# Wider exps, and a kernel's side work placed by a built-in time model: attention beside a state-space layer on one core

## The chip, the cores and the metric

One core of one Trainium2 chip. The metric is the device time of one launch in microseconds (us), median of several runs. The engines are TensorE (PE in the profile; PEld its weight loads), VectorE (DVE), ScalarE (ACT), GpSimd (POOL) and SyncE (SP), which in this kernel issues nearly all DMAs. SPq, PEq and so on are the engines' instruction queues.

Kernel before: 1026.12 us.

## The reference

```python
x = A_x                                              # 1 x 2048 x 512, bf16
g = sigmoid((x * gate_w).sum(-1, keepdims=True))
a = attention(x, wqkv, wo)                           # 32 heads of 16, softmax over 2048 keys, then @ wo
b = s4_conv(x, A, B, C, log_dt, Dskip)               # 512 channels x 128 complex states, length 2048
return g * a + (1 - g) * b
```

Attention is dominated by the exps: 32 x 2048 x 2048 of them, on 128 partitions 1,048,576 columns. ScalarE does them all. The convolution (called the SSM below) is done in blocks of 64 steps: tables of powers (VectorE), block states ("S stage", TensorE), a scan over 32 blocks (VectorE), outputs ("y stage", TensorE). Its operands travel through HBM between the stages.

## The kernel before

The kernel is built in Python: a recorder (`Prog`) takes instructions in the order given to each engine and works out the semaphores. Engines run their own list strictly in that order. Attention is the frame; the SSM, the projections and the output product are generators whose pieces are put between its steps.

```python
def qk(q):                       # scores: 4 matmuls of 32 rows, into two 2-bank PSUM buffers of three
    slots = [(SC[((4 * q + j) // 2) % 3], (4 * q + j) % 2) for j in range(4)]
    ...
def ex(h):                       # one exp over two banks, 1024 columns
    op("ACT", lambda a: a.activation(ET(1024 * e, [[1, 1024]]), sc(0, [[1, 1024]]), AF.Exp, scale=DH ** -0.5), ...)
...
def sload(blk):                  # a DMA, and the flags that later work waits for while the program is built
    yield ("AFTER", f"S{blk}", 2)
    ...
    sch.mark(f"sg{blk}")
...
    yield ("AFTER", f"sg{4 * qr + bl}", 12)      # scan: 12 steps (22 us) after its load was issued
    yield ("AFTER", f"qt{blk}", 3)               # S stage: 3 steps more after its Qt load
    yield ("AFTER", f"yl{u}", 5)                 # y stage: 5 steps after its loads
...
for q in range(NQ):              # the frame: 512 steps of two exps
    ex(2 * q); qk(q + 1); ex(2 * q + 1)
    rate = dict(PE=.62 if q > 50 else 1.0, DVE=1.65, POOL=1.8)     # budget of side work in this step, us
    pv(...)                      # products of exps with V
    sch.step(rate)
```

The softmax here doesn't subtract the row's maximum and nothing guards it: scores larger than these inputs give would overflow.

## Time and profile before

| part of the 1027.0 us span | us | read from |
|---|---|---|
| until the first exp | 20.0 | timeline of ScalarE |
| 1024 exps x 0.917 | 939.0 | length of an unbroken run of exps |
| gaps between exps (waits for scores) | 43.7 | waits of ScalarE |
| two square roots with four table loads | 6.4 | timeline |
| slower first exps after gaps, rest | 6.8 | what is left |
| after the last exp | 11.2 | timeline |

The page of the kernel before: busy time and share of the span, and the 40-slice rows of ScalarE's share and TensorE's granted clock in tenths.

```profile
span 1027.0 us, 16317 instructions
...
PE 740.6 (72%) x6617; PEld 195.9 (19%) x6617; DVE 626.7 (61%) x1356; ACT 959.0 (93%) x1041; POOL 3.6 (0%) x11
...
ACT  4899999999999998999997987999999999999995
...
PEclk7998998555556555657555665555555555557856
...
L550 ACT ACTIVATE ET<-SC 128x1024 bf16<-128x1024 f32 x1024 | 944.8, 1097 | 44.7 <-PE SC L433 43.7
```

ScalarE is the limit: 93% busy, and the exps are nearly all of it. The last line reads: 1024 exps, 944.8 us busy in total, 1097 ns from start to end of one (they overlap, so an unbroken run costs 0.917 us each), 44.7 us of idle time before them, 43.7 of it waiting for score matmuls (`SC`). The clock is half for most of the span.

The next views of the kernel before are waits (engine, what it waited for, us in total, times, longest): ScalarE's first line.

```profile
ACT ET L550 <- PE SC L433: 43.7, 37, 3.4
```

### The profile page before, as it was taken

The numbers are of one execution on the slowest core, as the hardware profiler recorded it, in microseconds if no ns is written. First come the engines' busy times: TensorE is split into PE (matmuls) and PEld (weight loads), VectorE is DVE, ScalarE is ACT, GpSimd is POOL, SyncE is SP. The second block draws the span as 40 slices with busy tenths as digits, with TensorE's granted clock in tenths as the row PEclk, the third lists the DMA queues.
The fourth block names the chain that finished last, engine by engine and source line by source line (L and its number), as shares of the span: only waits on it lengthen the run. The fifth ranks groups of instructions, "written<-read, shape, count | busy, mean of one in ns | idle before, by whom it ended". The sixth has DMA issues, their size and how long they took to land.

```text
span 1027.0 us, 16317 instructions
## 1 busy us (share of the span) xinstructions
PE 740.6 (72%) x6617; PEld 195.9 (19%) x6617; DVE 626.7 (61%) x1356; ACT 959.0 (93%) x1041; POOL 3.6 (0%) x11
## 2 busy tenths in 40 slices
PE   5876766766776666676665667888878888877665
PEld 1211111211111111111111112232322222311111
DVE  6737889997567897766897632112999971122111
ACT  4899999999999998999997987999999999999995
POOL 0000000000000000000000000000000000000000
PEclk7998998555556555657555665555555555557856
DMA  8610000006667205459104475458454444200000
GB/s 179 138 28 1 1 1 1 1 1 176 191 192 169 88 1 113 152 146 211 41 1 136 137 193 128 107 106 170 118 127 88 97 96 110 53 14 26 21 11 21
DMA packets 227403, 92.17 MB, mean 90 GB/s; under 512 B 191872, under 2 KB 215040, under 8 KB 225280
## 3 DMA queue, kind: packets, MB, share of 16 engines
q1 hardware_dynamic: 225600, 90.21, 35.5%
q10 hardware_dynamic: 1728, 0.92, 0.5%
q8 instruction: 52, 0.85, 0.4%
q14 instruction: 23, 0.19, 0.1%
HBM read 27.92 MB, written 35.65 MB: 62 GB/s over the span
## 4 chain that ended last, share of the span: by engine, by line
ACT 61%; DVE 21%; PE 12%; SPq 3%; issue 2%; DMA 1%; DVEq 0%; POOL 0%; POOLq 0%
ACT ET L550 60%; PE MB L433 6%; PE SC L433 4%; DVE G L887 3%; PE OA L433 2%; DVE s L885 2%; DVE s L882 2%; DVE s L880 2%; DVE SG L889 2%; DMA gm_sd<-Sst 1%; SPq L787 1%; DVE VE L516 1%; DVE OT L565 1%; DVE VE L481 1%; SPq L911 1%
## 5 line engine op out<-in xcount | busy, mean ns | idle before, releaser
L550 ACT ACTIVATE ET<-SC 128x1024 bf16<-128x1024 f32 x1024 | 944.8, 1097 | 44.7 <-PE SC L433 43.7
L433 PE MATMUL SC<-Qm,KT 32*128 32x512 bf16 x2048 | 289.2, 555 | 210.8 <-ACT ET L550 206.6
L433 PE MATMUL OA<-ET,VE 128*32 128x512 bf16 x2048 | 286.2, 563 | 0.1
L433 PEld LDWEIGHTS SC<-Qm,KT 32*128 32x128 bf16 x2048 | 54.5, 97 | 411.4 <-ACT ET L550 394.2
L433 PEld LDWEIGHTS OA<-ET,VE 128*32 128x32 bf16 x2048 | 53.8, 101 | 188.4 <-issue 183.8
L947 DVE CAST Yst<-MB 128x256 bf16<-128x256 f32 x32 | 13.5, 421 | 116.1 <-PE MB L433 116.1
L834 DVE CAST Sst<-MB 128x256 bf16<-128x256 f32 x64 | 27.0, 422 | 61.9 <-PE MB L433 51.6
L575 DVE TENSOR_TENSOR tt<-B,D 128x1024 bf16<-128x1024 bf16 x96 | 62.0, 687 | 1.2
L433 PE MATMUL MB<-Qt,X 64*32 64x256 bf16 x512 | 39.1, 397 | 31.5 <-DVE Sst L836 26.7
L565 DVE STREAM_TRANSPOSE OT<-OA 128x512 f32<-128x512 f32 x32 | 22.9, 714 | 62.4 <-PE OA L433 62.2
L887 DVE TENSOR_TENSOR G<-s,s 128x256 f32<-128x256 f32 x120 | 51.0, 425 | 4.1
L880 DVE TENSOR_TENSOR s<-G,MU 128x256 f32<-128x256 f32 x120 | 50.1, 417 | 0.1
L882 DVE TENSOR_TENSOR s<-G,MU 128x256 f32<-128x256 f32 x120 | 50.1, 418 | 0.0
L885 DVE TENSOR_TENSOR s<-s,SG 128x256 f32<-128x256 f32 x120 | 50.1, 418 | 0.0
L433 PE MATMUL MB<-Py,SG 128*32 128x64 bf16 x1024 | 44.3, 260 | 1.4 <-issue 1.4
L1036 DVE SCALAR_TENSOR_TENSOR fo<-MB,g,Yl 128x512 bf16<-128x512 f32 x13 | 9.7, 748 | 51.8 <-PE MB L433 51.8
L433 PE MATMUL MB<-Tt,X 64*32 64x64 bf16 x512 | 35.7, 269 | 3.3 <-DVE Yst L947 3.3
L889 DVE CAST SG<-G 128x256 bf16<-128x256 f32 x120 | 35.2, 294 | 4.1
L575 DVE TENSOR_TENSOR PT<-tt,tt 128x1024 bf16<-128x1024 bf16 x48 | 33.2, 692 | 1.6
L575 DVE TENSOR_TENSOR ft<-FP,L 128x1024 f32<-128x1024 f32 (+1 forms) x32 | 33.7, 1085 | 0.4
L810 DVE CAST Kst<-MB 128x512 bf16<-128x512 f32 x16 | 11.0, 689 | 36.9 <-PE MB L433 36.9
L433 PE MATMUL MB<-xT,Wk 128*128 128x512 bf16 x64 | 22.5, 440 | 15.2 <-DVE xT L1078 8.0
(115 smaller groups left out, 430.5 us busy)
## 6 DMA issues: line engine op xcount, KB each, us to landing
gm_ptd<-PT SPq DMA_DIRECT2D x16, 1024.0 KB, 5.0
Py<-gm_ptd SPq DMA_DIRECT2D x32, 512.0 KB, 4.6
gm_sd<-Sst SPq DMA_DIRECT2D x64, 128.0 KB, 2.4
gm_kpd<-Kst SPq DMA_DIRECT2D x16, 256.0 KB, 2.6
Tt<-gm_kpd SPq DMA_DIRECT2D x128, 32.0 KB, 3.7
gm_xrd<-in_A_x_dram SPq DMA_DIRECT2D x1, 2048.0 KB, 12.3
X<-gm_xrd SPq DMA_DIRECT2D x8, 256.0 KB, 4.8
gm_ytd<-Yst SPq DMA_DIRECT2D x32, 64.0 KB, 1.8
```

The lines of the kernel that those rows point to most:

```text
L433: op("PE", lambda t: t.matmul(out(), lhsT(), rhs(), start=start, stop=stop, skip_group_check=True, **kw), R, W)
L550: op("ACT", lambda a: a.activation(ET(1024 * e, [[1, 1024]]), sc(0, [[1, 1024]]), AF.Exp, scale=DH ** -0.5), [(sc, 0, h // 2), (sc, 1, h / ...
L565: op("DVE", lambda v: v.transpose(OT(o, [[1, 512]]), OA(0, [[1, 512]])), [(OA, 0, b)], [(OT, 0, b)])
L575: op(eng, lambda v: v.tensor_tensor(o(), a(), b_(), f), R, W)
L810: op("DVE", lambda v: v.tensor_copy(Kst(1024 * (blk % 2) + 63, [[P, 8], [1, T]]), MB(0, [[T, 8], [1, T]])), [(MB, 0, ('K', blk)), (Kst, "z ...
L834: op("DVE", lambda v, bank=bank: v.tensor_copy(Sst(512 * bank, [[256, 2], [1, 128]]), MB(0, [[256, 2], [1, 128]])), [(MB, 0, ('S', blk, ba ...
L880: op(e, lambda v: v.tensor_tensor(s2(0, [[128, 2], [1, 128]]), G(0, [[128, 2], [1, 128]]), MU(d0, [[0, 2], [1, 128]]), ALU.mult), key("G", ...
L882: op(e, lambda v: v.tensor_tensor(s3(0, [[128, 2], [1, 128]]), G(128, [[-128, 2], [1, 128]]), MU(D + d0, [[D, 2], [1, 128]]), ALU.mult), k ...
L885: op(e, lambda v, so=so: v.tensor_tensor(s2(0, [[128, 2], [1, 128]]), s2(0, [[128, 2], [1, 128]]), sg(so, [[RS, 2], [1, 128]]), ALU.add), ...
L887: op(e, lambda v: v.tensor_tensor(G(0, [[1, 256]]), s2(0, [[1, 256]]), s3(0, [[1, 256]]), ALU.add), [(s2, 0), (s3, 0)], [(G, 0)])
L889: op(e, lambda v, so=so: v.tensor_copy(sg(so, [[RS, 2], [1, 128]]), G(0, [[128, 2], [1, 128]])), key("G"), ks)
L947: op("DVE", lambda v: v.tensor_copy(Yst(r2 * 256, [[1, 256]]), MB(0, [[1, 256]])), ky, [(Yst, r2, u)])
```

## The change

Its intent: fewer, wider exps (three banks at a time, two buffers of three banks in place of three of two); side work placed by a time model in the builder that asks what is ready and fits before the next scores; dummy matmuls that keep TensorE's clock up; the first 24 tiles of exps kept in a spare buffer, so that scores need not wait for V; V's ones written by GpSimd; square roots by Newton steps on VectorE, so that ScalarE loads no other table. The diff is 1,656 lines; its core:

```diff
-    sb("ET", 7 * 1024)
+    sb("ET", NE * 1536)                 # NE = 6
+    sb("EX", NX * 1536)                 # NX = 18
...
-    for i in range(3):
-        B[f"SC{i}"] = Buf(f"SC{i}", "ps", 1024, FP32)
+    for i in range(2):
+        B[f"SC{i}"] = Buf(f"SC{i}", "ps", 1536, FP32)
...
+    def put(self, o):                   # the time model: when does o run on its engine?
...
+        t = self.free[eng]
+        for d, j in deps.items():
+            t = max(t, self.te[(d, j)] + (.03 if d == eng else LAT))
+        if o.dma:
+            self.free[eng] = t + .12    # time that issuing a DMA takes
+            e = t + o.c                 # time at which it has landed
...
+    def run(self, now, pe_end, dve_end, margin=.02):     # place ready work until the next scores are due
...
+    def keep(b):                        # a dummy: adds zeros to the open product
+        return mm(lambda: OA(0, [[1, 512]]), lambda: wm(0, [[1, P]]), lambda: wm(0, [[1, 512]]), [(wm, 0)], [(OA, 0, b)],
+                  False, False, c=.24)
...
-        yield ("AFTER", f"qt{blk}", 3)
...
-                yield ("AFTER", f"sg{4 * qr + bl}", 12)
+                yield ("AFTER", f"sg{4 * qr + bl}")
...
-            yield ("AFTER", f"yl{u}", 5)
+            yield ("AFTER", f"yl{u}")
...
+        while opened and sch.units < 3.2 and p.free["PE"] + .3 < lim:
+            put(keep((pvn - 1) // 16))
+            sch.units += 1
```

## The prediction

> **What bounds it now.** ScalarE. The page gives it 959.0 of 1027.0 us (93%), 944.8 of that in 1024 exps of 128x1024; the chain that ended last is 60% exps. In the timeline 52 exps in a row take 47.84 us: 0.917 us each. At 1.2 columns per ns (853 ns), about 64 ns of it are fixed (estimate). The rest of the span: the first exp starts at 19.98 us; the last ends near 1015.8 (tail 11 us); 44.7 us are idle before exps in 37 gaps, nearly all put down to the score matmuls (waits view); two square roots with four table loads of 1.28 us take 6.4 us.
>
> **What the change does.**
> 1. Exps of 1536 columns: 682, and one of 1024. At 1280 + 64 = 1.344 us each: 917 us, against 1024 x 0.917 = 939. Saves 22 us, all on the critical path. An exp after a gap costs up to 0.18 us more, so fewer gaps save 4 to 6.
> 2. Square roots on VectorE: ScalarE saves 6.4 us. VectorE gains some 22 operations of about 0.65 us (14 us), but loses the 7.53 us fill of V's buffer and a second pass over each S bank (64 x 0.41 us). It is 61% busy: off the path.
> 3. Head: the V fill holds VectorE from 3.2 to 10.7 us, so the copies of x and the decay inputs start late (ScalarE idles 7.15 us before the `ea` exp). With ones from GpSimd I expect the first exp at 14.5 to 15.5 us: saves about 5.
> 4. Gaps. The early ones (20 to 60 us, about 5 us) come from V projections ahead of scores; with 24 score tiles buffered, most go. Later ones (2.4 to 3.5 us before S-stage matmuls whose inputs or eviction are late; 1.1 to 1.7 us at state, output and projection work) come from in-order TensorE work that delays the next scores. A period becomes 1.344 us with 3 score matmuls, and only ready work is placed in it. The order of instructions shows SSM and output work ending by score 1638 of 2048 (before: 1976), so it makes no tail.
> 5. 1006 dummy matmuls hold the TensorE clock up. At 500 to 550 us the granted clock is 0.50 and 4 score matmuls take 0.61 us; at 50 to 150 us it is 0.9 and they take 0.39. The Trainium skill, "TensorE: Matmul & The Clock Gate", Part 1, says activity in 3.4 us windows lifts the clock from half to full; this trace agrees (stretch means 0.50 to 0.94). At half clock, scores, products and two dummies would need about 4 x 0.43 = 1.7 us per 1.344 us tile, dense enough to lift it. I expect a mean clock above 0.85 and TensorE no bottleneck.
>
> **Sum.** First exp 15 + exps 917 + gaps 13 (4 to 40) + gate and restarts 1 + tail 11 = 957 us. Range 944 to 985. Chances: faster by over 2% 0.96, within 2% 0.03, slower 0.01.
>
> **What would show each step.** Exps: 683, busy 917 to 922 us, spacing 1.344; no square-root tables on ScalarE; first exp near 15 us; idle before exps under 20 us; clock over 0.85 in the middle; no SSM work in the last 200 us.
>
> **What would make it wrong.** The clock falling although dummies run (1.7 us tiles); an optimistic time model whose late DMAs or evictions block TensorE in order, so gaps stay at 40 us; GpSimd fills slowing VectorE in the head.

## More of the kernel before

```profile
PE SC L433 <- ACT ET L550: 206.6, 387, 3.5
PE MB L433 <- DVE Sst L836: 26.7, 19, 3.8
...
PE MB L433 <- DMA Qt<-gm_ptd: 2.1, 1, 2.1
```

TensorE waits mostly for ScalarE to free score buffers, which costs nothing. It waited for a DMA of the SSM once, for 2.1 us.

The view of one line, the `Tt` loads of the y stage in the kernel before: duration of an issue on SyncE (minimum/median/maximum, ns), who waited, and the time to landing.

```profile
L911 SPq DMA_DIRECT2D Tt<-gm_kpd x128: 583/617/1778, 603.9 to 881.5; - x128
...
who waited for it (us, times):
...
DMA to landing us min/median/max: 2.4/3.7/5.5
```

Each of these loads holds SyncE for 0.617 us. Nobody waited for one.

## The result

The changed kernel takes 1020.06 us (1019.48 to 1022.12, 4 runs) against 1024.96 us for the kernel before in the same job. The ratio is 0.9956 (95% interval 0.9933 to 0.9979). Ratios here and below are those on record, taken from the fast runs of one job, so not quite the ratio of the medians quoted. That is 0.4% faster, and 63 us above the prediction.

The page of the changed kernel, lines as before.

```profile
span 1017.4 us, 17925 instructions
...
PE 890.5 (88%) x7623; PEld 261.4 (26%) x7623; DVE 605.8 (60%) x1315; ACT 934.6 (92%) x694; POOL 8.4 (1%) x17
...
ACT  6999999999799999699999964899897999999996
...
PEclk9999989989799999889788965699795999999999
...
L681 ACT ACTIVATE ET<-SC 128x1536 bf16<-128x1536 f32 x665 | 902.8, 1598 | 68.1 <-PE SC L547 67.4
```

The exps are wider and fewer, the clock is high, the head is full. But idle time before exps grew from 44.7 to 68.1 us, and the holes in ScalarE's row lie in the middle, while the SSM runs.

The waits of the changed kernel, ScalarE's first line and TensorE's first four:

```profile
ACT ET L681 <- PE SC L547: 67.4, 74, 9.9
```

```profile
PE SC L547 <- ACT ET L681: 49.6, 120, 1.3
PE MB L547 <- DMA Tt<-gm_kpd: 24.5, 20, 9.4
PE MB L547 <- DVE Sst L937: 13.8, 12, 5.9
PE MB L547 <- DMA Qt<-gm_ptd: 5.9, 4, 2.3
```

TensorE now waits 30.4 us for DMAs of the SSM, where before it was 2.1. Its list is in order: while a y or S matmul waits for its load, the scores behind it wait too. The longest wait for `Tt`, 9.4 us, is the longest gap between exps, 9.9 us. Timeline of TensorE and ScalarE there (start, length, engine, line, what; in brackets the idle time before):

```profile
608.73 2.79 ACT L681 ACTIVATE ET<-SC 128x1536 bf16<-128x1536 f32 x2
...
619.39 0.26 PE L547 MATMUL MB<-Tt,X 64*32 64x64 bf16 x1 [9.42 <-DMA Tt<-gm_kpd]
...
620.78 0.61 PE L547 MATMUL SC<-Qm,KT 32*128 32x512 bf16 x3
...
621.44 1.45 ACT L681 ACTIVATE ET<-SC 128x1536 bf16<-128x1536 f32 x1 [9.92 <-PE SC L547]
```

And SyncE's own queue over the same stretch:

```profile
606.12 0.60 SPq L1050 DMA_DIRECT2D gm_ytd<-Yst  x1
606.77 7.34 SPq L960 DMA_TRANSPOSE SG<-gm_sd  x3
614.16 0.60 SPq L1004 DMA_DIRECT2D Py<-gm_ptd  x1
614.80 2.69 SPq L1009 DMA_DIRECT2D Tt<-gm_kpd  x4
```

SyncE was issuing three `SG` transposes for 7.34 us, then `Py`, then the four `Tt` loads for which TensorE stood still. Nothing is idle in this list: each issue follows the last within 0.1 us. The model had charged 0.12 us for each of them. The DMA engines were full too in these microseconds (a mean share of 1.02 from 600 to 621 us), but that is not what TensorE waited for: the four loads landed 3.5 to 4.6 us after their issues, as loads do elsewhere (below). TensorE had stood since 609.97 us, 4.8 us before the first of them was issued.

The second longest gap (6.3 us, ending at 433.5 us) comes from SyncE's list by way of another engine. Four `SG` transposes took SyncE 11.88 us; VectorE stood 7.92 us before a step of its scan that reads them, and the eviction (`Sst`) that an S matmul waited for stood behind that step in VectorE's list.

The view of the changed kernel's `Tt` line says who waited for those loads, and how fast they are:

```profile
L1009 SPq DMA_DIRECT2D Tt<-gm_kpd x128: 603/617/1674, 558.7 to 780.1; - x128
...
  PE MB L547: 24.5, 20
...
DMA to landing us min/median/max: 2.4/3.6/5.5
```

The loads are as quick as before, from issue to landing (3.6 against 3.7 us) and in the issue itself (617 ns in both). They were issued too late for the place that the program gives to the work on them.

| part of the span | before | predicted | after |
|---|---|---|---|
| until the first exp | 20.0 | 15 | 15.2 |
| exps | 939.0 | 917 | 917.5 |
| gaps between exps | 43.7 | 13 | 66.0 |
| square roots | 6.4 | 0 | 0 |
| first exps after gaps, gate, rest | 6.8 | 1 | 9.8 |
| after the last exp | 11.2 | 11 | 8.9 |
| sum | 1027.1 | 957 | 1017.4 |

The exps of the changed kernel are counted as 682 x 1.344 + 0.917 us; an exp after a gap shows 1.45 us, 0.106 more than 1.344, and 73 gaps of that are 7.7 of the 9.8. Of the 67.4 us in the view of waits, 1.4 lie before the first exp and are counted there. The gain on everything but the gaps and restarts, 35 us, is close to the predicted one. Of it, 25 us were given back as gaps and restarts in this profiled run.

I sorted the gaps by summing the timeline: 15 of 1 us or more sum to 40.1 us, 59 smaller ones to 27.3 (the one before the first exp included). (Before: 22 and 15, 37.0 and 6.8.) The small ones come mostly in trains behind a large one, as after the wait for `Qt` at 259 us:

```profile
259.64 0.65 PE L547 MATMUL MB<-Qt,X 64*32 64x256 bf16 x8 [2.31 <-DMA Qt<-gm_ptd]
...
264.59 1.03 PE L547 MATMUL OA<-wm 128*128 128x512 bf16 x2
265.56 0.61 PE L547 MATMUL SC<-Qm,KT 32*128 32x512 bf16 x3
266.10 0.62 PE L547 MATMUL OA<-ET,VE 128*32 128x512 bf16 x4
266.22 1.45 ACT L681 ACTIVATE ET<-SC 128x1536 bf16<-128x1536 f32 x1 [0.60 <-PE SC L547]
```

After the block the scores take 0.61 us (half clock) where they take 0.39 at full clock, and the two dummies `OA<-wm` in front of them take 1.03. A tile with scores, products and two dummies then needs about 2.05 us of TensorE from start to start (its matmuls overlap a little, so this is less than the sum of their lengths) against 1.45 us of ScalarE for an exp after a gap, so each such tile leaves a gap of 0.6 us until the clock is back.

### The profile page after: what moved, and what is told of

Read it like the earlier page. It is cut to its first block, busy times and chain, and to the rows that moved or that the text cites. A ratio compares the mean times of both kernels' runs of the same rounds, so it can differ in the third digit from the quotient of the medians.

```text
span 1017.4 us, 17925 instructions
## 1 busy us (share of the span) xinstructions
PE 890.5 (88%) x7623; PEld 261.4 (26%) x7623; DVE 605.8 (60%) x1315; ACT 934.6 (92%) x694; POOL 8.4 (1%) x17
## 4 chain that ended last, share of the span: by engine, by line
ACT 50%; PE 17%; DVE 15%; SPq 10%; DMA 5%; issue 1%; ACTq 0%; DVEq 0%
ACT ET L681 48%; PE OA L547 8%; PE SC L547 5%; PE MB L547 4%; SPq L1009 3%; DVE tt L712 3%; ACT EX L681 2%; DMA Qt<-gm_ptd 2%; SPq L960 2%; SPq L899 2%; DMA Tt<-gm_kpd 2%; DVE G L987 2%; DVE Sst L937 1%; DVE s L981 1%; DVE s L985 1%; DVE PT L712 1%
## 5 line engine op out<-in xcount | busy, mean ns | idle before, releaser
L681 ACT ACTIVATE ET<-SC 128x1536 bf16<-128x1536 f32 x665 | 902.8, 1598 | 68.1 <-PE SC L547 67.4
L547 PE MATMUL OA<-wm 128*128 128x512 bf16 x1015 | 324.6, 409 | 1.2 <-DVE wm L606 1.2
L547 PE MATMUL OA<-ET,VE 128*32 128x512 bf16 x1994 | 212.1, 420 | 0.0
L547 PEld LDWEIGHTS SC<-Qm,KT 32*128 32x128 bf16 x2048 | 67.0, 92 | 357.1 <-ACT ET L681 281.2
L547 PEld LDWEIGHTS OA<-wm 128*128 128x128 bf16 x1015 | 65.7, 99 | 132.6 <-issue 118.6
L937 DVE TENSOR_TENSOR Sst<-MB,sgn 128x512 bf16<-128x512 f32 x64 | 43.9, 686 | 65.9 <-PE MB L547 39.1
L1048 DVE CAST Yst<-MB 128x256 bf16<-128x256 f32 x32 | 13.5, 423 | 64.6 <-PE MB L547 59.5
L547 PE MATMUL MB<-Qt,X 64*32 64x256 bf16 x512 | 31.5, 326 | 18.7 <-DVE Sst L937 12.3
L547 PE MATMUL MB<-Tt,X 64*32 64x64 bf16 x512 | 25.1, 246 | 25.4 <-DMA Tt<-gm_kpd 24.5
L547 PE MATMUL MB<-Py,SG 128*32 128x64 bf16 x1024 | 29.6, 244 | 0.0
L547 PEld LDWEIGHTS MB<-Tt,X 64*32 64x32 bf16 x512 | 15.7, 145 | 48.5 <-DMA Tt<-gm_kpd 32.7
```

What stands on the lines that cost most here:

```text
L547: return O("PE", lambda t: t.matmul(out(), lhsT(), rhs(), start=start, stop=stop, skip_group_check=True, **kw), R, W, c, l, u)
L681: return ac(lambda a: a.activation(b(1536 * e, [[1, 512 * n]]), sc(0, [[1, 512 * n]]), AF.Exp, scale=DH ** -0.5), [(sc, k, (t, k)) for k i ...
L937: yield [dv(lambda v, bank=bank: v.tensor_tensor(Sst(512 * bank, [[1, 512]]), MB(0, [[1, 512]]), sgn(0, [[1, 512]]), ALU.mult), [(MB, 0, ( ...
```

## Experiments

**Theory A**: the builder's model believes DMAs to have landed that SyncE has not yet issued, because it charges 0.12 us per issue; the work on them blocks TensorE in order. The small gaps are its aftermath. **Theory B**: TensorE simply has too much to do in a tile (dummies, small matmuls), whatever the DMAs do. **Theory C**: two score buffers give too little reserve, where three gave enough.

### e1: charge SyncE what an issue costs

```diff
-            self.free[eng] = t + .12
+            self.free[eng] = t + o.u
...
+    ISSUE = dict(xT=3.0, Qt=5.0, SG0=2.5, SG1=2.5, Yl=1.3, AreT=1.3, ...)
     def dma(eng, fn, R, W, c):
-        return O(eng, fn, R, W, c, dma=True)
+        return O(eng, fn, R, W, c, u=ISSUE.get(W[0][0].name, .64), dma=True)
```

> Only the builder's time model is changed: it now charges SyncE, which issues the DMAs, 0.64 us per plain DMA, 5.0 us per Qt transpose, 2.5 per SG transpose, 1.3 per Yl transpose, as the trace of the changed kernel shows, in place of 0.12. Theory A (TensorE blocks in order on DMAs that the model believed had landed; the small gaps that follow are its half clock after such a block): waits of TensorE for Tt and Qt fall from 30 us to under 8, idle before exps from 67 to 15-30 us, time 965-985 us. Theory B (TensorE has too much to do with dummies and small matmuls, whatever the DMAs do): gaps stay above 50 us, time within 1% of the changed kernel.

Measured: 977.6 us (976.4 to 981.0), ratio 0.9537 (0.9507 to 0.9568). ScalarE's and TensorE's waits in e1:

```profile
ACT ET L683 <- PE SC L547: 24.5, 41, 3.2
```

```profile
PE MB L547 <- DVE Sst L939: 12.2, 13, 3.4
PE MB L547 <- DMA Tt<-gm_kpd: 6.8, 8, 1.3
```

The wait for `Qt` is no longer among the costly ones, that for `Tt` fell from 24.5 to 6.8 us, the gaps from 67.4 to 24.5 (and 1.9 for a product). The edit makes no instruction of the kernel faster: it only changes places in the lists.

Theory A holds, and B, which said that the gaps would stay above 50 us, falls: TensorE still has all of its work (its last SSM or output piece inside the attention comes at score 1752 of 2048, in the changed kernel at 1638). C is not needed for most of the gaps either, as e1 keeps the two score buffers. The test does not hold the order fixed, though: with the new times the builder put about 2,570 of TensorE's 6,608 matmuls other than dummies into another place (a comparison of the lists in the two traces). (A second hunk of the edit only keeps the issue time, stored in `u`, from being counted as TensorE work.)

### e11: twice as many issues, the same bytes

```diff
-                    Tt(r * 512 + 256 * a, [[64, 4], [1, 64]], 64 * par, 64),
-                    kpd.dram(... + par * 9 * P, [[1, 64], [18 * P, 4], [1, 64]])),
+                    Tt(r * 512 + 256 * a + 128 * h, [[64, 2], [1, 64]], 64 * par, 64),
+                    kpd.dram(... + (par + 4 * h) * 9 * P, [[1, 64], [18 * P, 2], [1, 64]])),   # for h in range(2)
```

> The changed kernel with each Tt load cut into two of half the size: the same bytes, 128 more issues of about 0.62 us on SyncE, still counted as 0.12 us in the model. Theory A (SyncE's issue time makes the y stage's loads late): up to 2.5 us more per unit, 32 units, less what slack there is: 1060-1100 us, with Tt waits of TensorE of 70 us and more. Theory B (TensorE has too much to do): within 1% of 1020 us.

Measured: 1079.49 us (1074.24 to 1083.99), ratio 1.0511 (1.0478 to 1.0545). Waits of ScalarE and TensorE in e11:

```profile
ACT ET L681 <- PE SC L547: 129.6, 95, 10.7
```

```profile
PE MB L547 <- DMA Tt<-gm_kpd: 66.9, 63, 9.8
```

128 issues more, at 0.62 us 79 us of SyncE (an estimate from the median issue in the changed kernel), lengthened the program by 59 us and the waits for `Tt` by 42. The half loads landed sooner after their issues (2.8 us median in place of 3.6), so the transfers themselves did not slow down. SyncE's other issues kept their order; about 810 of TensorE's matmuls moved. The dose works in both directions.

### e2: the Tt loads issued by GpSimd

```diff
-                yield [dma("SP", lambda e, par=par, a=a: e.dma_start(
+                yield [dma("POOL", lambda e, par=par, a=a: e.dma_start(      # with semaphores of their own
```

(A first build, in which they shared semaphores with SyncE's loads, was not sound.)

> The 128 Tt loads are issued by GpSimd in place of SyncE; the model's 0.12 us and nearly all of the order stay. Theory A: SyncE's queue loses 0.64 x 4 of about 4.5 us per y unit, so the Tt waits (24.5 us) mostly go, the Qt and S waits before 550 us stay: idle before exps 30-45 us, time 985-1000. Theory B: no change. A third possibility: GpSimd issues so slowly that the waits only move: no gain or a loss.

Measured: 1008.04 us (1001.63 to 1009.27), ratio 0.9816 (0.9776 to 0.9856), "unclear" at the threshold of 2%. The gain over the changed kernel is there, but less than expected (ScalarE still waited 54.8 us for scores, 30 to 45 were expected). TensorE's waits in e2:

```profile
PE MB L553 <- DVE Sst L943: 14.4, 10, 4.5
PE MB L553 <- DMA Py<-gm_ptd: 13.5, 7, 7.2
PE MB L553 <- DMA Qt<-gm_ptd: 5.6, 3, 2.9
```

`Tt` is gone from the head of the list, and `Py`, which stayed on SyncE and which nobody had waited for noticeably, took its place with 13.5 us: behind a repaired resource the next late load shows. It is no clean test: the order changed in a few places too, and GpSimd was busy 86.9 us with it (8.4 before).

### e3, e5, e10: leave the dummies out

The same cut in three orders: the dummies are timed by the model and not emitted, so that everything else keeps its place (for e3 I compared the lists of TensorE, VectorE, ScalarE and SyncE with the changed kernel's: equal but for the dummies).

```diff
     def put(self, o):
...
+        if o.u == 1.25:                 # a dummy
+            ...
+            self.free[eng] = t + o.c
+            return
...
-                  False, False, c=.24)
+                  False, False, c=.24, u=1.25)
```

> The same order on every engine, with the 1006 dummy matmuls left out (the first nine stay). If the dummies do what they are for: clock falls from 0.91 to about 0.6, idle before exps grows, time 1030 or more. If after each block they cost more than they bring (2-3 dummies at half clock make a 1.7 us tile): the small gaps (27 us in 59 gaps) shrink, the big ones (40 us) stay, time 1000-1015.

> The order of e1 with the 1003 dummy matmuls left out. e3 made 1015 us of the changed kernel's 1020 by the same cut, so if the dummies are worth nothing once late DMAs are rare, the time is 970-985 us at a clock near 0.6. If they are what keeps the undisturbed stretches free of gaps: 990 us or more.

> The order of e6 with its dummy matmuls left out. e5 against e1 showed the dummies to be worth nothing, so 963-971 us at a clock near 0.6, equal to e6 (968.2) within 0.5%. If in an order with few blocks the high clock does close the small gaps: 975 or more.

| order of | with dummies, us | without, us | clock with | without |
|---|---|---|---|---|
| the changed kernel (e3) | 1020.06 | 1015.10 | 0.906 | 0.589 |
| e1 (e5) | 977.6 | 977.09 | 0.947 | 0.599 |
| e6 (e10) | 968.17 | 967.74 | 0.955 | 0.587 |

The dummies do what they are for, and the time does not move. In the changed order it even falls by 0.5% (ratios to the kernel before 0.9956 and 0.9902, from different jobs); the small gaps shrank from 27.3 to 16.5 us, while the big ones grew from 40.1 to 44.9 and the wait for `Tt` stayed (24.6 us in place of 24.5). So a TensorE with 1,006 matmuls less to do in the same order has the same big gaps, which speaks against theory B once more. These runs change the dummies and the clock together; what a high clock alone would be worth is not separated. Why the pair is worth nothing is seen in a quiet stretch. Busy time in 850 to 950 us (length, PE, PEld, DVE, ACT, POOL, then clock, DMA share, GB/s), first e3, then the changed kernel:

```profile
850.00:950.00 100.00, 75.43 (x449) 14.05 (x445) 7.12 (x17) 100.00 (x76) 0.00 (x0) 0.50 0.00 1
```

```profile
850.00:950.00 100.00, 88.38 (x601) 22.33 (x598) 5.66 (x13) 99.78 (x75) 0.00 (x0) 0.98 0.00 1
```

At half clock and without dummies ScalarE is 100.00 of 100 us busy. Scores of 0.61 us and products of 0.62 us fit into 1.344.

### e4 and e8: exps over two banks in three buffers

```diff
-W3 = 3
+W3 = 2
+NB = 3
-NE = 6
-NX = 18
+NE = 8
+NX = 24
...
-        sc, sl = SC[t % 2], tile(t)
+        sc, sl = SC[t % NB], tile(t)
...
-            put(*fill(t + 2))
+            put(*fill(t + NB))
```

with buffers, deadlines and dummy budget scaled to the narrower tile. e4 has the model of the changed kernel with its dummies; e8 has e1's issue times and no dummies.

> Exps over two banks in three buffers as before the change, everything else of the change kept (time model with 0.12 us DMA issue, dummies, early buffers of the same bytes, Newton roots). Theory A: the same late DMAs block TensorE, so gaps stay near 60-70 us, and exps cost 939 in place of 917 us: 1035-1050 us. Rival C (two score buffers have too little reserve, and that makes the gaps): gaps fall to 30-45 us and the time is at or below that of the changed kernel.

> Two-bank exps in three buffers, with e1's issue times and without dummies (e4 showed that they swamp TensorE there). This prices the three-bank exps: their 939 against 917 us of ScalarE should show as 20-30 us against e5, so 993-1010 us. If three buffers of two banks save more in gaps than the wide exps bring: 985 or less.

e4 measured 1347.65 us, ratio 1.3194. All my expectations were wrong, and it tests neither A nor C: TensorE became the limit. Its busy time in 500 to 550 us:

```profile
500.00:550.00 50.00, 49.97 (x207) 8.90 (x206) 30.18 (x64) 34.10 (x35) 0.00 (x0) 0.50 0.25 82
```

TensorE is busy 49.97 of 50 us, and the clock stays at 0.50. That run is still useful: it contradicts what my prediction said of dense work lifting the clock (below).

e8 measured 1025.80 us, ratio 1.0004 (0.9975 to 1.0034); 993 to 1010 was expected. Against e5 (977.09 us, same job) the two-bank form costs 48.7 us. ScalarE's busy time differs by 31.2 of it (963.9 against 932.7 us): the 22 us of the narrower exps, and slower starts. The rest is gaps and a longer wait at some places (39.4 + 5.6 against 25.9 + 0.5 us idle before exps), 8.8 us of it one wait for a product. So the wide exps bring at least the 22 us, and three buffers of two banks did not do better on gaps: theory C found no support. How much of the 18.6 us of extra gaps belongs to the form and how much to deadlines that I scaled by hand is not separated.

### e6: a margin on landing times

```diff
-            e = t + o.c
+            e = t + o.c * (1.4 if self.q > 100 else 1.0)        # on e1
```

> e1, and from the hundredth exp on the model takes every DMA's landing 1.4 times as long, so that work on its data is placed later. Theory A: what is left of e1's gaps (24.5 us) are late stores and loads and the half-clock tiles after them; idle before exps falls to 8-15 us, time 958-968 us. If e1's leftover has another cause: within 0.5% of e1 (977.6).

Measured: 968.17 us (965.77 to 973.29), ratio 0.9449 (0.9410 to 0.9487). ScalarE's waits in e6:

```profile
ACT ET L683 <- PE SC L547: 16.2, 24, 2.8
```

Gaps fell from 24.5 to 16.2 us, slightly above the 8 to 15 expected, while the time came out in the range. What is left is three gaps of over 1 us and their trains; the largest, 2.8 us, is an S matmul that waits for an eviction (`Sst`), as is the largest in e1 (3.2 us). Three such evictions in e1 had themselves waited for the store of the block before it to leave the buffer (5.61, 1.48 and 4.22 us of idle VectorE ended by `DMA gm_sd<-Sst` in e1), so a late DMA again, a store this time. A larger ring for `Sst` was not run.

### e9: square roots back on ScalarE

```diff
-        yield from rsqrt("u3", "u1", "u2")
-        yield [tt(full("u3"), full("u3"), full("u1"), ALU.mult, key("u3", "u1"), key("u3"))]
+        yield [O("ACT", lambda a: a.activation(B["u3"](0, [[1, D]]), B["u1"](0, [[1, D]]), AF.Sqrt), key("u1"), key("u3"), 3.1)]
```

(on e1; likewise for the second root, with a reciprocal on VectorE)

> e1 with the two square roots back on ScalarE (and one reciprocal of 3.3 us on VectorE in place of the Newton steps). The table loads and roots cost 6.4 us of ScalarE: 982-986 us against e1's 977.6, 0.5 to 0.9% more. If ScalarE had slack there: no difference.

Measured: 984.94 us (976.70 to 986.09), ratio 0.9579 (0.9531 to 0.9627) against e1's 0.9537 (0.9507 to 0.9568). ScalarE is busy 938.7 us in place of 931.2. The busy time shows the expected cost of about 7 us; the timed difference points the same way, but the intervals overlap, and the builder ordered the side work anew here too (ScalarE's waits for scores are 27.3 us in place of 24.5), so the run agrees and doesn't prove it.

## Why the prediction was wrong

It said 957 us, 944 to 985, and 0.96 for faster by over 2%. It was 1020.06.

1. *Exps of 1536 columns: right.* Predicted 683 at 1.344 us. In the changed kernel a run of 43 takes 57.87 us; less the 1.45 of the first, that is 56.42 over 42, 1.343 us each. The 512 columns more cost 0.426 us, which is the 1.2 columns per ns that the prediction had assumed.
2. *Square roots: right.* No table is loaded after the first exp. VectorE stayed at 60%.
3. *Head: right.* 15.18 us for the first exp (14.5 to 15.5 predicted), 1.2 us of gaps between exps before 200 us (before: 8.9).
4. *Gaps: this is the step that failed.* "Only ready work is placed in it" was taken over from the code without asking whether "ready" in the builder was ready on the chip. The term "gaps 13 (4 to 40)" measured 66.0, and the restarts that follow gaps, put at 1, 9.8. e1 changed just the model's issue time and took 42 us off the time; e11 added issues and put 59 on. What would have told: the diff shows `.12` for an issue, and the trace of the kernel before shows 0.617 us for a `Tt` load and 5.1 us (median) for a `Qt` transpose; the change also removed the fixed distances behind DMAs. In the y stage one unit has a `Py` load, four `Tt` loads and a store, and every second one a transposed read: 0.60 + 2.59 + 0.60 + 0.63 = 4.4 us of SyncE from the changed kernel's timeline, where the model counted 6.5 x 0.12 = 0.8. I had named "an optimistic time model whose late DMAs or evictions block TensorE in order" as a risk, and bounded it at 40 us without costing it.
5. *Dummies and clock: half right, and worth nothing.* The mean clock was 0.906, above the 0.85 predicted. But "dense enough to lift it" was wrong: in e4 TensorE was busy 49.97 of 50 us at a clock of 0.50. The trace of the kernel before, which I had called agreeing, has both levels of the clock but does not show busy time to set them: TensorE was busy 43.73 of 50 us at 0.50 (650 to 700 us) and 34.96 of 50 at 0.89 (50 to 100 us). And the clock, which I let stand as the condition for small gaps, is not one where the dummies are left out too: e3, e5 and e10 run at 0.59 to 0.60 and lose nothing.
6. *Tail: right.* 8.9 us (11 predicted); SSM and output work end well before.

The best version run is e6's order: 968 us, with dummies or without, 5.5% below the kernel before (5.8% for e10, ratio 0.9420, interval 0.9401 to 0.9438, in another job).

## What to carry to other kernels

A placement by a time model is as good as its worst constant: check each one, and first the issue time of DMAs on the queue that carries most of them, against the trace that you already have. In an engine that runs in order, one late operand stops all that stands behind it, so work on DMA data wants a margin (a factor of 1.4 on landing brought another 1% here). Before paying for a higher TensorE clock, look whether the work at half clock already fits into the limiting engine's period.

## What the Trainium skill lacked or had wrong

- "DMA: Bandwidth & Descriptors", section "Issuing engines are not separate DMA queues": the sequencer's time to initiate a DMA "is usually small relative to the DMA itself". Here a 32 KB load held SyncE for 0.617 us of 3.6 us to landing, about a sixth, but a `Qt` transpose for 5.0 of 8.2 us (medians of the changed kernel). In the longest gap SyncE's queue, and not the DMA engines, set when the y stage's loads came.
- "TensorE: Matmul & The Clock Gate", Part 1, ties the clock to how busy TensorE has been in windows of about 3.4 us. It doesn't say what counts as busy: in e4 TensorE was busy 49.97 of 50 us by the profile and had a clock of 0.50, while the changed kernel, 88.38 of 100 us busy, had 0.98. What tells the two apart is open.
- "ScalarE: Activation LUTs", section "What ACT_TABLE_LOAD costs": 1283 ns for a table load agrees with this trace (1283). Its numbers for an ACTIVATE with immediate scale and bias (186 ns + 0.833 ns per column, 93 ns of overlap when back to back) give 93 + 1280 = 1373 ns at 1536 columns (estimate from that page); measured 1343 for the exps from PSUM here.
